# Turning q and k with SBUF-to-SBUF transfer transposes instead of on TensorE, with their casts one period earlier

## The chip, the cores and the metric

One core of one Trainium2 chip. The metric is the device time of one execution in microseconds (us). Before the change it was 352.41 us, the median of three runs (351.92 to 353.83). Runs over 1.5% above the fastest of the same kernel count as slow and are kept out of the ratios.

## The reference, cut to what matters

Attention of 8 heads over 8 batches of 576 tokens, with a window of 32 tokens to each side plus 8 global tokens, then a token-mixing and a channel-mixing MLP:

```python
scores = scale * np.matmul(q, k.transpose(0, 1, 3, 2))        # q, k, v: (8, 8, 576, 64) f32
mask = (np.abs(pos[:, None] - pos[None, :]) <= 32) | is_global[:, None] | is_global[None, :]
attn = softmax(np.where(mask, scores, -1e9));  x = attn @ v    # heads joined: (8, 576, 512)
h  = np.maximum(xt @ w_tok1, 0.0) @ w_tok2;    u = x + h.transpose(0, 2, 1)
h2 = np.maximum(u @ w_ch1, 0.0) @ w_ch2;       return u + h2   # w_ch1: 512 x 1536
```

## The kernel before

The work is cut into periods. In the period of batch b TensorE runs the channel MLP of b (the fixed work, `M4` and `M5`). Between its pieces it ends the attention of b+1 (`PV`, `M1`, `M2`, `M3`), and turns and scores q and k of b+2.

A score needs q and k with the head dimension on the partitions, while the load puts tokens there. So each pair of heads is loaded in f32, cast to f16 on ScalarE, turned on TensorE into PSUM (`T`), and copied by VectorE into token order (`TE`):

```python
def T(b, p):
    pT = (psm if b in (0, 2) else pss)([P, 2, 512], F16, name=f"pT_{b}_{p}")
    for ti, n in enumerate((qn, kn)):
        for i in range(4):
            nc.tensor.transpose(out=pT[:, ti, P*i : P*i+P], in_=n[b % 2][:, i, 2*p : 2*p+2, :], identity=ident)
    st[b]["pT", p] = pT
```

The load buffers `lq` and `lk` are single, the casts' outputs `qn` and `kn` double. The MLP's PSUM pool `psm` has two buffers, and ScalarE empties each with a Relu:

```python
def M4(b, j):                       # 12 groups of four matmuls per period
    ps = psm([P, 512], name=f"b1p_{b}_{j}")
    ... four matmuls ...
    nc.scalar.activation(out=s["b1"][:, j, :], in_=ps, func=AF.Relu)
```

And one queue, SyncE's, carries the q and k loads, the transposes of the MLP's input (`M3`) and the outputs:

```python
# first_half(b): n = b + 1, m = b + 2;  D is one piece of the fixed MLP work
u = [D, D, pv(0), D, pv(1), *c(0), D, pv(2), *c(1), D, pv(3), ..., *c(2), D]      # c(k): two casts of batch m
u += [pv(4), TR(m), *tt(0), *c(3), D, M1(n, 3), D, M1(n, 4), *c(4)]               # tt(p): T and TE of batch m
u += [load_v16(m), v_odd(m), globals_(m)]
u += [load_rest(m + 1), load_qk(m + 1)]                                           # used a period later
u += [*tt(1), D, D, M2(n, 0), M3(n, 0), D, M2(n, 1), M3(n, 1), *tt(2), D, M2(n, 2), ..., D]
```

The softmax here doesn't subtract the row's maximum and nothing guards it: scores larger than these inputs give would overflow.

## Time and profile before

| | before |
|---|---|
| time of the profiled run, span | 352.01 us, 350.2 us |
| mean granted TensorE clock (share of full speed that the chip allowed) | 0.984 |
| periods of batches 2, 3, 4, 5 | 38.0, 40.7, 35.6, 40.7 us |

A period is counted from the first MLP matmul (`b1p`) of a batch to that of the next. These two groups of the page are the ones to hold beside the changed kernel's (after the bar: busy us and mean ns of one, then the idle time ahead of the group and what ended it):

```profile
L739 PE MATMUL b1p<-uT,wc 128*128 128x512 f16 x384 | 95.6, 382 | 0.5 <-ACT b L742 0.5
...
L405 DVE COPY qT<-pT 128x512 f16<-128x512 f16 x30 | 20.6, 687 | 15.6 <-PE pT L399 15.4
```

Over the whole run TensorE waits 0.5 us for the Relu to empty a PSUM buffer. The Relu keeps up.

### The profile page before, as it was taken

Reading aid. Unit: us, or ns where it says so; the run is one execution under the profiler, and the core shown is the slowest. Engines: PE = TensorE matmul, PEld = TensorE weight load, DVE = VectorE, ACT = ScalarE, POOL = GpSimd, SP = SyncE. Lnnn points to the kernel's source line nnn. Section 1 sums busy time; section 2 is a strip of 40 time slices with the busy share of each in tenths; the row PEclk is TensorE's granted clock in tenths of the full one; section 3 lists DMA queues with packets and bytes.
Section 4 is the critical chain, followed back from the end, with each engine's and each line's share of the span. In section 5 each row is a group of like instructions: output and inputs, shape, how many; then the busy total and the mean of one; then the engine's idle time right before and its main releaser. Section 6 shows DMA issues by size and latency. Waiting matters only on the chain.

```text
span 350.2 us, 8086 instructions
## 1 busy us (share of the span) xinstructions
PE 319.4 (91%) x3431; PEld 174.0 (50%) x3431; DVE 190.4 (54%) x395; ACT 153.4 (44%) x275; POOL 86.8 (25%) x111
## 2 busy tenths in 40 slices
PE   4699998985899999799998999899989999999993
PEld 4357754443456544444454644444545645444641
DVE  7476576846742866456647475565656464241021
ACT  2460466025758044553475452554456433413600
POOL 5788686422126000520044001530000000000000
PEclk9999999997899999989999999999999999999999
DMA  6999999299857962929293922959100221042012
GB/s 199 216 155 263 249 128 70 92 226 204 255 60 70 256 139 65 93 60 287 92 89 56 257 92 66 96 162 214 62 2 19 73 72 52 0 105 92 0 68 86
DMA packets 82023, 42.38 MB, mean 121 GB/s; under 512 B 56578, under 2 KB 76674, under 8 KB 81986
## 3 DMA queue, kind: packets, MB, share of 16 engines
q1 hardware_dynamic: 44080, 31.34, 33.7%
q0 software_dynamic: 37904, 10.52, 28.1%
q8 instruction: 27, 0.44, 0.5%
q14 instruction: 10, 0.08, 0.1%
q10 hardware_dynamic: 2, 0.00, 0.0%
HBM read 36.11 MB, written 9.44 MB: 130 GB/s over the span
## 4 chain that ended last, share of the span: by engine, by line
PE 79%; DVE 8%; issue 5%; DMA 3%; ACT 2%; POOL 1%; SPq 1%; ACTq 0%
PE op L765 25%; PE b1p L739 23%; PE a1p L691 4%; PE pT L399 4%; PE hp L711 4%; PE s L457 4%; DMA lk<-in_k_dram 3%; PE b1lp L752 3%; PE pv L655 3%; PE pv L664 2%; DVE x L678 1%; PE a1p L612 1%; ACT e_all L469 1%; PE pv L586 1%; PE og L538 1%
## 5 line engine op out<-in xcount | busy, mean ns | idle before, releaser
L739 PE MATMUL b1p<-uT,wc 128*128 128x512 f16 x384 | 95.6, 382 | 0.5 <-ACT b L742 0.5
L742 ACT ACTIVATE b<-b1p 128x512 f16<-128x512 f32 x96 | 56.9, 598 | 88.1 <-PE b1p L739 87.9
L765 PE MATMUL op<-wc,b 128*128 128x512 f16 x384 | 89.3, 380 | 0.0
L469 ACT ACTIVATE e_all<-s 128x544 f16<-128x544 f32 (+1 forms) x64 | 41.0, 686 | 40.9 <-issue 30.5
L360 POOL DMA_DIRECT2D vsh<-in_v_dram x35 | 29.5, 853 | 118.2 <-PE pv L664 101.2
L765 PEld LDWEIGHTS <-b 128*128 128x128 f16 x384 | 35.3, 98 | 39.4
L739 PEld LDWEIGHTS <-wc 128*128 128x128 f16 x384 | 34.6, 98 | 37.4 <-issue 2.2
L769 DVE TENSOR_TENSOR osb<-u,op 128x512 f32<-128x512 f16 x32 | 22.0, 687 | 54.5 <-PE op L765 52.2
L405 DVE COPY qT<-pT 128x512 f16<-128x512 f16 x30 | 20.6, 687 | 15.6 <-PE pT L399 15.4
L716 DVE TENSOR_TENSOR u<-x,hp 128x1024 f16<-128x1024 f16 x14 | 17.0, 1220 | 21.3 <-PE hp L711 21.3
L677 DVE RECIPROCAL rr<-pv 128x8 f32<-128x8 f32 (+1 forms) x35 | 7.2, 206 | 33.3 <-PE pv L664 33.3
L480 DVE TENSOR_TENSOR e_all<-e_all,bandm 128x616 f16<-128x616 f16 x56 | 24.3, 475 | 1.0
L678 DVE TENSOR_TENSOR x<-pv,rr 128x512 f16<-128x512 f32 (+1 forms) x35 | 24.2, 691 | 1.2
L457 PE MATMUL s<-qT,kT 64*64 64x136 f16 (+2 forms) x704 | 19.4, 231 | 4.8 <-ACT kT L411 2.2
L457 PEld LDWEIGHTS <-kT 64*64 64x64 f16 x704 | 12.4, 114 | 19.2 <-issue 13.9
L411 DVE COPY kT<-pT 128x512 f16<-128x512 f16 x30 | 20.4, 680 | 1.5 <-PE pT L399 0.8
L711 PE MATMUL hp<-a,w 128*128 128x512 f16 x72 | 19.3, 386 | 1.5 <-ACT a L695 1.5
L399 PE MATMUL pT<-ident,qn 128*128 128x128 f16 x128 | 14.2, 241 | 6.9 <-DVE kT L437 6.3
L655 PE MATMUL pv<-rf,lf 128*64 128x264 f16 x126 | 18.9, 287 | 0.9 <-DVE kgz L354 0.7
L399 PE MATMUL pT<-ident,kn 128*128 128x128 f16 x128 | 14.5, 245 | 4.5 <-ACT kn L385 4.0
L664 PE MATMUL pv<-vsh,e_all 128*64 128x66 f16 x280 | 18.5, 194 | 0.0
L664 PEld LDWEIGHTS <-e_all 128*64 128x64 f16 x504 | 18.4, 111 | 0.0
(171 smaller groups left out, 383.8 us busy)
## 6 DMA issues: line engine op xcount, KB each, us to landing
out_dram<-osb SPq DMA_DIRECT2D x32, 256.0 KB
lq<-in_q_dram SPq DMA_DIRECT2D x6, 1024.0 KB
lk<-in_k_dram SPq DMA_DIRECT2D x6, 1024.0 KB
wc<-in_moe_w_ch_dram POOLq DMA_DIRECT2D x6, 512.0 KB, 7.7
vsh<-in_v_dram POOLq DMA_DIRECT2D x21, 128.0 KB, 5.0
vsh<-in_v_dram POOLq DMA_DIRECT2D x14, 96.0 KB, 3.0
lq<-in_q_dram SPq DMA_DIRECT2D x4, 256.0 KB
lk<-in_k_dram SPq DMA_DIRECT2D x4, 256.0 KB
```

What stands on the lines that cost most here:

```text
L360: nc.gpsimd.dma_start(out=vsh[b % 2][r0:r1, c, :, 0:D], in_=v[b, :, j0 : j0 + (r1 - r0), :].rearrange("h p d -> p h d"),)
L399: nc.tensor.transpose(out=pT[:, ti, P * i : P * i + P], in_=n[b % 2][:, i, 2 * p : 2 * p + 2, :], identity=ident)
L457: nc.tensor.matmul(ps[o, par, i0 - a : i1 - a], lhsT=kT[r, HQ * j : HQ * j + HQ], rhs=qf[r, i0:i1], start=b > 0, stop=b > 0 or j in js[-2:],)
L469: nc.scalar.activation(out=e2[:, :, a:z], in_=ps[:, :, 0 : z - a], func=AF.Exp, scale=scale)
L480: nc.vector.tensor_mul(out=e2[:, par], in0=e2[:, par], in1=bm)
L655: nc.tensor.matmul(ps[r0 : r0 + 64, hf, 0 : NP * VW], lhsT=s["lf"][:, HQ * t : HQ * t + HQ], rhs=s["rf"][:, 2 * hf : 2 * hf + 2], start=Tr ...
L664: nc.tensor.matmul(ps[r0 : r0 + 64, hf, VW * hh : VW * hh + VW], lhsT=e_all[:, h, lo : lo + HQ], rhs=(vod if t % 2 else vsh)[b % 2][:, tau ...
L678: nc.vector.tensor_tensor(out=x16s[b % 2][r, tau, :].rearrange("p (f h x) -> p f h x", f=2, h=NP), in0=pq[r, :, :, 0:D], in1=rr[r].unsquee ...
L711: nc.tensor.matmul(ps[:, i, :], lhsT=w2[:, ch, P * tau - sh : P * tau - sh + P], rhs=s["a1"][:, ch, :], start=(ch == 0), stop=(ch == 1),)
L739: nc.tensor.matmul(ps, lhsT=wc1[:, cc, P * j : P * j + P], rhs=s["uT"][:, cc, :], start=(cc == 0), stop=(cc == 3))
L742: nc.scalar.activation(out=s["b1"][:, j, :], in_=ps, func=AF.Relu)
L765: nc.tensor.matmul(ps, lhsT=w, rhs=wc2[:, j, :], start=(j == 0), stop=(j == NJ - 1))
```

## The change

For batches 4 to 7 the eight 128x128 transposes of a pair of heads leave TensorE. Eight DMA transposes per batch (`QT`) go from SBUF to SBUF instead, and VectorE puts the result in token order (`TS`). A transfer takes time to land, so the casts move from the period of the scores into the period ahead of it. The load behind them moves too, from the first half to the end of the second.

```diff
+    def QT(b, ti, i):
+        nc.sync.dma_start_transpose(
+            out=(qraw, kraw)[ti][:, :, i, :], in_=(qn, kn)[ti][b % 2][:, i].rearrange("p h d -> p (h d)"))
+    def TS(b, p):
+        nc.vector.tensor_copy(out=qTs[b % 2][:, p, 0:4, NG:QS]..., in_=qraw[:, p]...)
+        nc.vector.tensor_copy(out=kTs[b % 2][:, p, WIN : WIN + 512]..., in_=kraw[:, p]...)
 ... end of the stage before (sparse2) ...
+        u += [(0.0, c) for c in casts(n + 1)]
+        u += [(0.0, lambda ti=ti, i=i: QT(n + 1, ti, i)) for i in range(4) for ti in range(2)]
+        u += [(0.0, lambda: (load_rest(n + 2), load_qk(n + 2, slice(0, H))))]
 ... first_half(b) ...
-        cs = casts(m) if m < B else []
+        cs = casts(c_) if c_ < B else []          # c_ = b + 3
-            return [lambda: t(m, p)] if m < B else []
+            return [lambda: TS(m, p)] if m < B else []
-        if m + 1 < B:
-            u += [lambda: (load_rest(m + 1), load_qk(m + 1, slice(0, H)))]
 ... second_half(b) ...
-        return [D, s2(m, 0), D, lambda: t(m, 3), lambda: SM(m, 0), D, s2(m, 1), D, lambda: SM(m, 1), D, s2(m, 2), D, ...
+        return [D, *x(0), s2(m, 0), D, *x(1), lambda: SM(m, 0), D, s2(m, 1), *x(2), D, lambda: SM(m, 1), *x(3), D, s2(m, 2),
+                ld, D, ...                        # x(k): two QT of batch c_;  ld: the load of batch c_ + 1
```

More of the change, by code (lines that the diff above doesn't have):

```diff
@@ L418, in TE @@
         TEk(b, p)
+    qraw, kraw = [const.tile([P, NP, 4, P], F16, name=f"{n}raw") for n in "qk"]
+    def QT(b, ti, i):
+        nc.sync.dma_start_transpose(
+            out=(qraw, kraw)[ti][:, :, i, :], in_=(qn, kn)[ti][b % 2][:, i].rearrange("p h d -> p (h d)")
+        )
+    def TS(b, p):
+        nc.vector.tensor_copy(
+            out=qTs[b % 2][:, p, 0:4, NG:QS].rearrange("p t (x i) -> p t x i", i=4),
+            in_=qraw[:, p].rearrange("p i (t x) -> p t x i", t=4),
+        )
+        nc.vector.tensor_copy(
+            out=kTs[b % 2][:, p, WIN : WIN + 512].rearrange("p (x i) -> p x i", i=4),
+            in_=kraw[:, p].rearrange("p i x -> p x i"),
+        )
     def TR(b):
@@ L838, in first_half @@
     def first_half(b):
-        n, m = b + 1, b + 2
+        n, m, c_ = b + 1, b + 2, b + 3
         D = None
-        cs = casts(m) if m < B else []
+        cs = casts(c_) if c_ < B else []
         def c(k):
@@ L859, in first_half @@
             u += [lambda: (load_v16(m), v_odd(m)), lambda: globals_(m)]
-        if m + 1 < B:
-            u += [lambda: (load_rest(m + 1), load_qk(m + 1, slice(0, H)))]
         u += [*tt(1), D, D, lambda: (M2(n, 0), M3(n, 0)), D, lambda: (M2(n, 1), M3(n, 1)), *tt(2), D]
-        u += [lambda: (M2(n, 2), M3(n, 2) if n % 2 else None), D]
+        u += [lambda: (M2(n, 2), M3(n, 2) if n % 2 else None), D, *tt(3)]
         return u
     def second_half(b):
-        m = b + 2
+        m, c_ = b + 2, b + 3
         D = None
@@ L870, in second_half, with x, ld @@
             return []
-        return [D, s2(m, 0), D, lambda: t(m, 3), lambda: SM(m, 0), D, s2(m, 1), D, lambda: SM(m, 1), D, s2(m, 2), D,
-                lambda: SM(m, 2), lambda: GK(m), s2(m, 3), D, lambda: SM(m, 3), D, lambda: OG(m)]
+        def x(k):
+            return [lambda ti=ti: QT(c_, ti, k) for ti in range(2)] if c_ < B else []
+        def ld():
+            if c_ + 1 < B:
+                load_rest(c_ + 1)
+                load_qk(c_ + 1, slice(0, H))
+        return [D, *x(0), s2(m, 0), D, *x(1), lambda: SM(m, 0), D, s2(m, 1), *x(2), D, lambda: SM(m, 1), *x(3), D, s2(m, 2),
+                ld, D, lambda: SM(m, 2), lambda: GK(m), s2(m, 3), D, lambda: SM(m, 3), D, lambda: OG(m)]
     def dense(b):
```

## The prediction

> **What bounds the kernel now.** I read the page first, then the busy table by stage, the order of work on TensorE in one stage, and last ScalarE and the DMA queue of SyncE around the place where the change adds work.
>
> ```profile
> PE 319.4 (91%) x3431; PEld 174.0 (50%) x3431; DVE 190.4 (54%) x395; ACT 153.4 (44%) x275; POOL 86.8 (25%) x111
> PE 79%; DVE 8%; issue 5%; DMA 3%; ACT 2%; POOL 1%; SPq 1%; ACTq 0%
> ...
> 135.10:173.10 38.00, 35.66 (x378) 18.17 (x378) 23.13 (x49) 18.16 (x33) 8.07 (x7) 0.96 0.63 124
> 173.10:213.90 40.80, 39.29 (x439) 21.18 (x436) 23.49 (x44) 19.94 (x36) 8.08 (x7) 1.00 0.61 119
> 213.90:249.45 35.55, 33.89 (x376) 17.22 (x374) 21.54 (x42) 18.15 (x33) 8.07 (x7) 1.00 0.72 132
> 249.45:290.20 40.75, 39.24 (x435) 21.16 (x436) 21.92 (x44) 19.94 (x36) 0.00 (x0) 1.00 0.16 47
> ```
>
> TensorE holds the chain of waits (79%). The last four rows (length, busy of PE, PEld, DVE, ACT, POOL, clock, DMA share, GB/s) are the periods of batches 2 to 5, the ones that today turn q and k of batches 4 to 7. PE is idle in them for only 2.34, 1.51, 1.66 and 1.51 us. So only work or waits taken off TensorE can pay. Most of that idle time is one wait:
>
> ```profile
> 184.90 0.38 PE L399 MATMUL pT<-ident,qn 128*128 128x128 f16 x4 [1.51 <-DVE kT L437]
> 185.12 0.39 PE L399 MATMUL pT<-ident,kn 128*128 128x128 f16 x4
> 185.34 1.03 PE L739 MATMUL b1p<-uT,wc 128*128 128x512 f16 x4
> ```
>
> The first transposes of a batch wait for VectorE to empty the PSUM buffer of the rest rows, then four q and four k transposes hold PE from 184.90 to 185.34, 0.44 us.
>
> What the new order leans on, in the same trace:
>
> ```profile
> 132.67 1.27 ACT L469 ACTIVATE e_all<-s 128x544 f16<-128x544 f32 x2
> 136.21 0.60 ACT L742 ACTIVATE b<-b1p 128x512 f16<-128x512 f32 x1 [2.27 <-PE b1p L739]
> ...
> 139.07 0.40 ACT L382 CAST qr<-lqr 128x256 f16<-128x256 f32 x1
> 139.37 0.41 ACT L382 CAST kr<-lkr 128x256 f16<-128x256 f32 x1
> 140.15 0.60 ACT L742 ACTIVATE b<-b1p 128x512 f16<-128x512 f32 x1 [0.38 <-PE b1p L739]
> 140.64 0.61 ACT L385 CAST qn<-lq 128x512 f16<-128x512 f32 x1
> ```
>
> ```profile
> 139.49 0.70 SPq L120 DMA_DIRECT2D lqr<-in_q_dram  x1
> 140.29 0.65 SPq L120 DMA_DIRECT2D lkr<-in_k_dram  x1
> 154.34 0.41 SPq L116 DMA_DIRECT2D lq<-in_q_dram  x1
> 154.85 0.52 SPq L116 DMA_DIRECT2D lk<-in_k_dram  x1
> 157.01 6.02 SPq L728 DMA_TRANSPOSE uT<-u  x4
> ```
>
> ```profile
> 156.00:158.00 2.00, 1.00 0.97 284
> 158.00:160.00 2.00, 1.00 1.04 361
> 160.00:162.00 2.00, 1.00 1.10 349
> ```
>
> Casts and the Relu evictions of the MLP alternate on one in-order engine, so a cast that waits for its load holds up the evictions behind it. Today the load of 154.3 is used a period later (178.6), so it has 24 us. The last fence is that load on the wire (stretch, length, clock, DMA share, GB/s): some 350 GB/s until about 162. A DMA transpose takes 1.2 to 1.5 us of the SyncE queue.
>
> **What the Trainium skill says.**
> - "TensorE: Matmul & The Clock Gate", Part 4: PE-mode transpose, gives about 275 ns for a 128x128 transpose in a kernel. The rows here average 241 to 245 ns, but they are pipelined: 0.44 us for eight, 55 ns each. The 55 ns is what I remove.
> - "DMA: Bandwidth & Descriptors", Latency and other measured facts, has 261 GB/s and more for DMA transposes. This trace does not reach it: from 308 to 310, with transposes alone, it moves 130 GB/s, a 128 KB transpose per us or so. Issue sets the pace.
> - "VectorE: DVE Perf Modes", What auto-detection actually checks: a one-source copy with both sides in SBUF and even outer dimensions can take a two-port mode even with a step that is not 1. The f32 casts of that kind on VectorE (128x512) took 411 to 444 ns uncontended, against 680 to 687 for today's copies from PSUM. So I expect the new copies at 0.35 to 0.45 us.
> - "TensorE: Matmul & The Clock Gate", Why this matters for your kernels, warns of PE gaps over about 3 us. Here even the 1.66 us gap before 147.92 is followed by a granted clock of 0.50 for some 3.4 us (147.9 to 151.3), a loss of 1.7 us.
>
> **The change part by part.**
>
> Removed: 4 batches x 4 pairs x 8 transposes = 128 on TensorE. 16 groups x 0.44 us = 7.0 us of PE time, all in stages where PE sets the end. With them goes the wait of 1.5 us per period (1.51 in the row above; the next user of that PSUM buffer comes several us later): 4 x 1.5 = 6.0 us. Gross gain 3.3 us per period, 13 us in all.
>
> VectorE: 32 copies of 0.68 us from PSUM become 32 of about 0.4 us. VectorE is busy 23 of 38 us in these stages; worth nothing directly. Some will wait behind GpSimd's copies, as the copy of the global columns does now (1.73 us at 186.75 against 0.19 at 117.81); there are over 2 us of room before the next addition.
>
> ScalarE: the same casts, one period earlier. SyncE: 8 transposes more per period, 8 x 1.3 = 10.4 us of queue; the data, 1 MB at 130 GB/s, fits beside the rest.
>
> Moved, and this is the cost: loads. The load for a batch now stands on the SyncE queue behind the eight transposes of the batch before, while its casts are due early in the next period.
>
> At the end of the second stage: the last exponentials end at 133.94. The ten casts of batch 4 follow (2 x 0.3 + 8 x 0.51, start to start) to 138.7. Already the Relu of 136.21 slips to 138.8, so PE loses about 2 us, not yet counted since a longer stall follows. The transposes issue from 138.3 (all q casts done): 8 x 1.35 = 10.8, to 149.1. Then the two rest loads (0.75 + 0.65) and q and k (0.5 + 0.5): k issued by about 151.5. The load issued at 154.34 to 154.85 moved its 2.1 MB between 155 and about 162.3, so k landed some 7.2 us after the end of its issue; here that is 158.7. On ScalarE the cast of k of the first pair ends at 159.3, the Relu behind it at 159.9. TensorE has two PSUM buffers for the MLP: it fills them, then stands until about 153 (rest rows landed) and again until 159.9. The seventh MLP group (the one behind the second pair of casts) started at 148.93 before, in the chain of waits; it starts at 159.9, 11.0 later. Two long gaps cost another half-clock stretch of 1.7, as before the change; the later three transpose groups of this stage save 1.3. Period of batch 2: **+10.5**.
>
> Period of batch 3: its load leaves SyncE after eight transposes of the second half that themselves start after the five MLP transposes, some 4.3 us into that half. 4.3 + 8 x 1.3 + 2 outputs x 0.4 + loads 2.4 = 17.9 us in, where the half is about 13.3 long: 4.6 after the period's end. k lands at +11.8, its Relu is done at +13.0. The seventh MLP group stood at +12.25 (185.34): +0.75, less 1.3 of transposes, plus about 0.8 (half a chance of the 1.7 us clock loss): **+0.2**.
>
> Period of batch 4: no fifth MLP transpose, and the half is 3 us longer; the load leaves 1.3 before the end, k lands at about +6, when its cast is due. No stall: **-3.3**. Period of batch 5 has neither casts nor loads: **-3.3**.
>
> Sum: 10.5 + 0.2 - 3.3 - 3.3 = +4.1, so 352.4 becomes 356.5. I say 357, since every slip of the queue adds to it and none of the slack is counted twice.
>
> **The rivals.**
> 1. The loads come in time and the gross gain stays: 352.4 - 13.1 = 339. For it: DMA engines are idle half the time. Against it: the SyncE order itself, since the transposes need casts that cannot start before 133.9. I give it little.
> 2. The late load repeats in three periods rather than one and a bit, because transposes issue at 1.5 to 2.1 us (the four from 114.76 in the queue's order of time took 8.45): 8 x 0.5 = 4 us later each time, 361 to 364.
> 3. VectorE becomes the bound: strided copies slow, or stuck behind a transpose that has not landed. The transposes land some 5 us before their copies are due, and VectorE has 15 us idle per period. It would cost 1 to 3 us at most.
> 4. The first stall is shorter, transposes at 1.2 us and a load at 6.5: 2.5 less, 354, and with no stall for batch 3 about 352.
>
> **Range and chances.** The sum has one large positive term (8 to 14 us) and a sure negative one (6 to 8). That gives 351 to 363. Slower by over 2% needs over 359.5: the large term at its upper end, or rival 2; 0.28. Faster by over 2% needs rival 1: 0.05. Within: 0.67.
>
> **What would show it.** Right: PE waits in the early period of batch 2 released by the Relu on ScalarE, which idles for some 8 to 18 us on the loads of q and k; the stage from 135 about 10 us longer; the stages of batches 4 and 5 about 3.3 us shorter, with no wait on the rest rows' copy; copies at 0.35 to 0.45 us; transposes of q and k at 1.2 to 1.5 us of queue. Wrong: no ScalarE wait on a load in those stages (then near 339), or stalls of over 5 us in the periods of batches 3 and 4 too (then over 362).

## The result, and the profile after

The changed kernel took **369.67 us** (median of 4 runs, 366.47 to 371.78) against 353.12 us (4 runs, 351.92 to 354.13): ratio 1.0462, 95% interval 1.0359 to 1.0566, slower. A ratio here is the mean time of one kernel's fast runs over that of the other's of the same rounds, so it is not quite the ratio of the medians quoted. The prediction was 357, with 351 to 363 as its range: too low, and the result lies outside the range.

From the changed kernel's page, its busy line, its chain of waits by engine, and the MLP group:

```profile
PE 313.3 (85%) x3303; PEld 165.0 (45%) x3303; DVE 186.9 (51%) x395; ACT 153.8 (42%) x275; POOL 86.5 (23%) x111
...
PE 49%; DMA 19%; SPq 10%; DVE 8%; ACT 5%; issue 5%; POOL 1%; POOLq 0%; ACTq 0%; DVEq 0%
...
L756 PE MATMUL b1p<-uT,wc 128*128 128x512 f16 x384 | 101.0, 399 | 25.9 <-ACT b L759 25.8
```

There are 128 matmul records fewer, so TensorE has less work (313.3 us against 319.4). But its wait for the Relu went from 0.5 to 25.9 us, and the chain now runs 29% through transfers and SyncE's queue. The mean MLP matmul also rose, from 382 to 399 ns. The busy table by period of the changed kernel (batches 2 to 5; columns as in the prediction):

```profile
135.40:186.60 51.20, 36.76 (x350) 17.30 (x346) 24.37 (x49) 21.79 (x40) 8.15 (x7) 0.83 0.70 113
186.60:235.60 49.00, 40.62 (x402) 20.50 (x403) 21.02 (x44) 20.13 (x36) 8.08 (x7) 0.86 0.69 130
235.60:273.30 37.70, 34.00 (x344) 16.10 (x343) 20.27 (x42) 18.17 (x33) 8.08 (x7) 0.95 0.74 140
273.30:310.40 37.10, 37.10 (x403) 19.30 (x404) 21.05 (x44) 15.40 (x26) 0.00 (x0) 1.00 0.28 78
```

| period of batch | before | after | difference | predicted |
|---|---|---|---|---|
| 2 | 38.0 | 51.1 | +13.1 | +10.5 |
| 3 | 40.7 | 49.1 | +8.4 | +0.2 |
| 4 | 35.6 | 37.6 | +2.0 | -3.3 |
| 5 | 40.7 | 37.0 | -3.7 | -3.3 |
| sum | | | +19.8 | +4.1 |

The spans differ by 19.8 us (370.0 against 350.2), so these four periods hold all of it. The table also shows the only undisturbed one. In the last row TensorE is busy 37.10 of 37.10 us at clock 1.00: neither casts nor loads are left in that period, and the gain is there.

ScalarE in order of time shows the wait. The bracket is the idle time before the instruction and what ended it:

```profile
140.62 0.60 ACT L759 ACTIVATE b<-b1p 128x512 f16<-128x512 f32 x1 [0.62 <-PE b1p L756]
153.04 0.40 ACT L382 CAST qr<-lqr 128x256 f16<-128x256 f32 x1 [11.82 <-DMA lqr<-in_q_dram]
...
157.93 0.62 ACT L385 CAST qn<-lq 128x512 f16<-128x512 f32 x1 [2.96 <-DMA lq<-in_q_dram]
160.72 0.62 ACT L385 CAST kn<-lk 128x512 f16<-128x512 f32 x1 [2.17 <-DMA lk<-in_k_dram]
161.25 0.59 ACT L759 ACTIVATE b<-b1p 128x512 f16<-128x512 f32 x1
...
204.83 0.62 ACT L385 CAST kn<-lk 128x512 f16<-128x512 f32 x1 [3.84 <-DMA lk<-in_k_dram]
```

The Relu of 161.25 has long had its input. It stands behind casts that wait for a load. Until it is done the MLP's two PSUM buffers stay full, and TensorE stands (2.59 us before its group of 161.89). The last line is the same thing a period later. Why the loads are late is on SyncE's queue (start, duration of the issue):

```profile
138.52 1.21 SPq L423 DMA_TRANSPOSE qraw<-qn  x1
...
148.54 1.26 SPq L423 DMA_TRANSPOSE kraw<-kn  x1
...
151.79 0.57 SPq L116 DMA_DIRECT2D lk<-in_k_dram  x1
...
192.73 1.77 SPq L116 DMA_DIRECT2D lk<-in_k_dram  x1
...
236.46 0.57 SPq L116 DMA_DIRECT2D lk<-in_k_dram  x1
```

Eight transposes hold the queue from 138.52 to 149.80, and only then the loads go. From the end of k's issue to the start of its first cast it takes 8.4 us (152.36 to 160.72), then 10.3 (194.50 to 204.83), then 11.2 (237.03 to 248.25).

A third cost follows each stall. One MLP group of TensorE after the second stall, then the busy table of the stretch it starts:

```profile
206.00 1.87 PE L756 MATMUL b1p<-uT,wc 128*128 128x512 f16 x4 [6.20 <-ACT b L759]
```

```profile
206.00:211.90 5.90, 5.90 (x14) 2.08 (x14) 0.00 (x0) 4.17 (x8) 3.89 (x2) 0.50 0.06 4
```

Four matmuls take 1.87 us instead of some 1.03, and TensorE is busy all of 5.90 us at a granted clock of 0.50: about 3 us lost. The stretch after the first stall (161.9 to 167.6) loses another 2.9 in the same way. The clock had fallen before these stretches: to 0.50 at about 150.5, in the first long wait, and at about 198.3, after a wait of 2.18 us and before the second long one.

### The profile page after: what moved, and what is told of

It reads as the page before. It is cut to its first block, busy times and chain, and to the rows that moved or that the text cites.

```text
span 370.0 us, 7857 instructions
## 1 busy us (share of the span) xinstructions
PE 313.3 (85%) x3303; PEld 165.0 (45%) x3303; DVE 186.9 (51%) x395; ACT 153.8 (42%) x275; POOL 86.5 (23%) x111
## 4 chain that ended last, share of the span: by engine, by line
PE 49%; DMA 19%; SPq 10%; DVE 8%; ACT 5%; issue 5%; POOL 1%; POOLq 0%; ACTq 0%; DVEq 0%
PE op L782 18%; DMA lk<-in_k_dram 18%; PE b1p L756 16%; SPq L423 6%; PE a1p L708 3%; PE hp L728 3%; PE b1lp L769 3%; PE s L474 3%; DMA lv<-in_v_dram 2%; SPq L120 2%; PE pv L672 1%; ACT kn L385 1%; ACT e_all L486 1%; SPq L116 1%; PE pv L681 1%
## 5 line engine op out<-in xcount | busy, mean ns | idle before, releaser
L756 PE MATMUL b1p<-uT,wc 128*128 128x512 f16 x384 | 101.0, 399 | 25.9 <-ACT b L759 25.8
L756 PEld LDWEIGHTS <-wc 128*128 128x128 f16 x384 | 36.2, 101 | 69.0 <-issue 34.9
L782 PEld LDWEIGHTS <-b 128*128 128x128 f16 x384 | 35.5, 98 | 40.3
L474 PE MATMUL s<-qT,kT 64*64 64x136 f16 (+2 forms) x704 | 18.3, 224 | 7.8 <-DVE kT L411 3.0
L385 ACT CAST kn<-lk 128x512 f16<-128x512 f32 x25 | 15.6, 623 | 14.6 <-DMA lk<-in_k_dram 14.6
L474 PEld LDWEIGHTS <-kT 64*64 64x64 f16 x704 | 12.0, 111 | 21.1 <-issue 13.3
L385 ACT CAST qn<-lq 128x512 f16<-128x512 f32 x25 | 15.5, 619 | 13.6 <-DMA lq<-in_q_dram 13.6
L372 POOL COPY vod<-vsh 64x2112 f16<-64x2112 f16 x6 | 11.7, 1945 | 27.2 <-DMA vsh<-in_v_dram 27.2
L708 PE MATMUL a1p<-x,w 128*128 128x512 f16 x56 | 15.7, 408 | 0.0
## 6 DMA issues: line engine op xcount, KB each, us to landing
wc<-in_moe_w_ch_dram POOLq DMA_DIRECT2D x6, 512.0 KB, 11.1
```

What stands on the lines that cost most here:

```text
L385: eng(out=(qn, kn)[ti][b % 2][:, :, hs].rearrange("p i h d -> p h i d"), in_=(lq, lk)[ti][:, hs])
L474: nc.tensor.matmul(ps[o, par, i0 - a : i1 - a], lhsT=kT[r, HQ * j : HQ * j + HQ], rhs=qf[r, i0:i1], start=b > 0, stop=b > 0 or j in js[-2:],)
L708: nc.tensor.matmul(ps[tt], lhsT=w, rhs=x16s[b % 2][:, ch, :], start=(ch == 0), stop=(ch == NT - 1))
L756: nc.tensor.matmul(ps, lhsT=wc1[:, cc, P * j : P * j + P], rhs=s["uT"][:, cc, :], start=(cc == 0), stop=(cc == 3))
L782: nc.tensor.matmul(ps, lhsT=w, rhs=wc2[:, j, :], start=(j == 0), stop=(j == NJ - 1))
```

## The experiments

All twelve kernels computed the right result except one. Its output is wrong, which doesn't matter for the time. The profiled runs of the first, the fourth and the sixth (`e1`, `e4`, `e6`) fell in the slow state, so of `e1` and `e4` only the kind of wait is read, not the last microsecond. "Median" is of all runs, slow ones too; the ratios use fast runs alone, so compare by them. Periods are those of batches 2 to 5, from the profiled run.

| run | median (n) | before | ratio, 95% | periods 2 to 5 |
|---|---|---|---|---|
| e1_load_first | 362.93 (4) | 352.28 | 1.0169, 1.0016 to 1.0323 | 44.6 44.4 36.8 37.0 |
| e2_pe_turn_same_order | 360.06 (5) | 352.28 | 1.0196, 1.0073 to 1.0319 | 39.2 45.2 35.6 40.6 |
| e3_v_later | 371.27 (4) | 352.28 | 1.0464, 1.0305 to 1.0624 | 52.5 47.1 36.1 37.0 |
| e4_casts_late | 371.89 (4) | 352.28 | 1.0508, 1.0407 to 1.0610 | 44.3 50.2 42.1 37.0 |
| e5_turn_ahead_of_loads | 342.80 (6) | 351.26 | 0.9766, 0.9730 to 0.9801 | 34.5 38.5 34.6 37.0 |
| e6_pe_turn_casts_late | 351.58 (12) | 351.26 | 1.0004, 0.9970 to 1.0038 | 36.4 40.6 35.5 40.6 |
| e7_no_v (wrong result) | 365.70 (4) | 351.26 | 1.0384, 1.0315 to 1.0453 | 52.1 46.7 34.8 37.0 |
| e8_loads_on_act | 348.61 (17) | 351.26 | 0.9907, 0.9879 to 0.9935 | 44.1 37.9 33.1 37.0 |
| e9_keep_clock | 370.47 (4) | 351.26 | 1.0554, 1.0501 to 1.0608 | 51.8 48.2 36.7 37.0 |
| e10_copies_later | 339.83 (6) | 351.26 | 0.9688, 0.9648 to 0.9727 | 33.4 37.0 34.0 37.2 |
| e11_keep_clock_shorter | 367.13 (6) | 351.25 | 1.0438, 1.0381 to 1.0495 | 49.2 47.3 35.3 37.0 |
| e12_changed_again | 372.06 (6) | 352.40 | 1.0544, 1.0472 to 1.0615 | 52.3 49.8 36.4 37.0 |

My theory on reading the result: the loads are late because they stand on SyncE behind the transposes, and ScalarE's in-order casts carry that delay to TensorE. The rivals: the casts at their new place are dear by themselves, the v loads make the q and k loads slow to land, or most of the loss is TensorE's clock.

### e1: the loads ahead of the transposes

```diff
-        u += [QT(n + 1, ti, i) ...];  u += [load of n + 2]
+        u += [load of n + 2];  u += [QT(n + 1, ti, i) ...]
-        return [D, *x(0), s2(m, 0), ..., s2(m, 2), ld, D, ...
+        return [D, ld, *x(0), s2(m, 0), ..., s2(m, 2), D, ...
```

> The changed kernel with one edit: the loads of q and k for the batch after next are issued ahead of the eight transposes instead of behind them (end of the second stage, and start of each second half). My theory: the loss is the in-order wait of ScalarE's casts for loads that leave SyncE 10 us too late. Then the stalls of the periods of batches 3 and 4 vanish (they become some 37.5 and 32.2 us long), that of batch 2 shrinks by 8 to 10 us, and the time is 342 to 347 us. Rival A, the transposes themselves load the DMA engines and delay every load whatever the order: over 358. Rival B, the strided copies on VectorE hold the scores: no change, about 369.

It took 362.93 us (ratio 1.0169). The loss fell, but nowhere near what was expected. Among the waits from 180 to 232 (engine, tile and line, what it waited for: us in total, times, longest) are new ones:

```profile
DVE osb L786 <- DMA out_dram<-osb: 8.0, 2, 6.0
...
PE b1p L756 <- DVE osb L786: 5.4, 1, 5.4
```

Outputs share the queue, so with a big load ahead of them they leave late. Their three buffers then stay taken, VectorE waits for one, and TensorE waits for VectorE. The first transpose behind the load took 4.97 us to issue instead of 1.2. This is in keeping with the Trainium skill, "DMA: Bandwidth & Descriptors", Queues, rings and completion order: SyncE's issues share one row of rings, each consumed in order. So the loads' place matters, and moving them forward moves part of the wait. The expectation missed this.

### e2: the same order, TensorE turning

```diff
-            return [lambda: TS(m, p)] ...    and all QT
+            return [lambda: t(m, p)] ...     # T and TE on TensorE and VectorE, as before the change
```

> As the run above (loads first, casts one period ahead), but q and k of batches 4 to 7 are turned on TensorE with the copies from PSUM as in the kernel before; no SBUF transfer transposes of q and k. It measures what moving the transposes is worth by itself. My theory: 13 us slower than the run above (3.3 us per period of PE work and the wait on the rest rows' copy), so 355 to 360. Rival A, transfer transposes cost as much as they save: the same as the run above within 2 us.

360.06 us, not slower than e1 beyond the noise (1.0196 against 1.0169), where 13 us were expected. The period of batch 3 took 45.2 us without one q or k transfer transpose on the queue; there too VectorE waited for outputs to leave (3.6 us, and TensorE behind it 2.9). So the early load at that place is harmful by itself, whoever turns q and k, and the pair cannot measure what the transposes' move is worth; e5 and e6 do.

### e3: the v loads later

```diff
-            u += [lambda: (load_v16(m), v_odd(m)), lambda: globals_(m)]
+            u += [lambda: globals_(m)]                         # v moved to the start of second_half(b)
```

> The changed kernel with only the loads of v and their shifted copies moved from the first half to the start of the second half, away from the late loads of q and k. In the changed kernel k landed 8.9, 12.1 and 11.8 us after its issue instead of the 7.2 I reckoned with. If the v loads (small packets on the other queue) are what slowed it, k lands some 7.5 to 8.5 us after issue and the time falls by 5 to 10 us to 360 to 365. If the transposes ahead of it in the same queue slowed it, landing stays near 12 and the time within 2 us of 369.

371.27 us, no change. It tested nothing: the v loads are issued by GpSimd when their buffer comes free, and they went at about the same time (191.61 to 199.67, against 189.62 to 199.67 in the changed kernel). e7 is its replacement.

### e4: the casts late, the load and then the transposes at the end of the period

```diff
-        u = [..., *c(0), ..., *c(1), ...]                     # no casts in the first half
+        return [D, s2(m, 0), *cs(0), D, ..., *cs(4), D, ..., OG(m), ld, *x()]   # casts, load, eight QT
```

> The transfer transposes kept, but the casts of the next batch moved from the first half into the second half, loads next and transposes last, so that each load has a whole half period before its casts. My theory: no ScalarE wait on a load is left in the stages from batch 2 on, the gross gain of 13 us shows, less 1 to 3 us for the casts of batch 4 at the seam: 339 to 344. Rival A or B: at or over 352.

371.89 us. ScalarE no longer waits for q and k, yet nothing was won. Of the waits from 132 to 300:

```profile
DVE qT L428 <- DMA qraw<-qn: 33.0, 4, 12.5
...
PE hp L728 <- DVE u L733: 26.7, 3, 11.2
```

The wait went to the other end of the same queue. The transposes stand behind a load (the first took 4.84 us to issue), VectorE's copies wait for them, and the additions behind those copies hold up TensorE. Whichever of the two comes second on the queue is late for its in-order consumer.

### e5 and e6: transposes ahead of loads, and both with a period's time

Casts late as in e4, but the transposes go at the very start of the next period and the loads right behind them. So the load has until the second half before its casts are due. e6 is the control: the same order with TensorE turning.

```diff
+        def q8():
+            eight QT(m, ...)                    # e6: none
+            load_rest(c_); load_qk(c_)
-        u = [D, D, pv(0), D, pv(1), *c(0), ...
+        u = [q8, D, D, pv(0), D, pv(1), D, ...
+        u += [D, *tt(0), D, *tt(1), M2(n, 0), ...]     # tt: TS in e5, t in e6 (e6 keeps the old places)
```

> What the run with late casts showed: ScalarE no longer waited, but VectorE did, because the transposes stood behind 2 MB of loads in the same queue (single issues of 4.8 to 5.5 us). So here: casts of the next batch in the second half (those of batch 4 spread between the last scores of the second stage), the eight transposes at the start of the next period when no output transfer is due, and the loads behind them with some 10 us left before their casts. My theory now: any order in which neither ScalarE waits for a load, nor VectorE for a transpose or an output buffer, shows the whole gain: the periods of batches 2 to 5 are some 34.7, 37.4, 32.2 and 37.0 us against 38.0, 40.7, 35.6 and 40.7, and the time 338 to 343. Rival (transfer transposes cost somewhere else what they save): 350 or more.

> The same order of casts and loads as the run above, but q and k turned on TensorE with the copies from PSUM. If the gain of the run above comes from the transposes taken off TensorE, this one takes 350 to 354, with periods within 0.7 of those before the change. If it came from the new places of casts and loads, this one is as fast as the run above.

e5: 342.80 us. e6: 351.58, the same as before the change. So the new order alone is worth nothing (1.0004), the casts' place in the second half costs nothing, and the transposes' move is worth 8.8 us between these two. The time of e5 is at the upper end of what was expected: its periods of batches 3 and 4 took 38.5 and 34.6 us, not 37.4 and 32.2. e10 takes that up.

### e7: no v loads (wrong result)

```diff
-            u += [lambda: (load_v16(m), v_odd(m)), lambda: globals_(m)]
+            u += [lambda: v_odd(m), lambda: globals_(m)]
```

> The changed kernel with the loads of v left out from batch 4 on (wrong result on purpose: old rows of v are used). My run that moved them later in program order left them at the same times, so it did not test this. If the small packets of v slow the loads of q and k, k lands 7 to 8.5 us after the end of its issue in the periods of batches 3 and 4 (12.1 and 11.8 in the changed kernel), and the time falls to 358 to 364. If they do not, landing stays at 11 to 12 and the time at 367 to 371.

365.70 us, a relative error of 0.89, and between the two forecasts. (The 12.1 and 11.8 us of the expectation count from the start of k's issue, not from its end.) Counted so, k took 11.1 and 10.5 us to its cast in the periods of batches 3 and 4, about 1 us less than with the v loads. In that of batch 2 it took 10.5 against 8.9, so longer. That is no more than two profiles of one kernel differ. From the end of k's issue, e7 shows 9.9, 10.5 and 9.9 us, the changed kernel 8.4, 10.3 and 11.2, and the same kernel in e12 10.0, 13.0 and 10.6. The time's ratio, 1.0384, lies below the changed kernel's 1.0462 and 1.0544, but its interval (1.0315 to 1.0453) overlaps that of the first (from 1.0359). So the v loads may cost a little time, but that they slow k's landing is not shown, and what did is left open.

### e8: the changed kernel, its late loads on ScalarE's queue right behind the casts

```diff
-        ... s2(m, 2), ld, D, ...                                # second half, SyncE, behind eight QT
+        u += [lambda: (load_rest(c_ + 1, nc.scalar), load_qk(c_ + 1, slice(0, H), nc.scalar))]   # behind c(4)
```

> The changed kernel with the late loads issued from ScalarE's queue right behind the casts that free their buffer, so that they pass the SyncE queue with its eight transposes; everything else as changed. If SyncE's order is the cause, the stalls of batches 3 and 4 vanish and that of batch 2 shrinks by 8 us: 343 to 350. What may stay is the wait of output buffers behind the transposes (up to 2 us per period). If loads and transposes only share the wires, so that order does not matter: 360 or more.

348.61 us. Casts, transposes and copies are those of the changed kernel; only where the loads stand differs, on the other queue and so much earlier. k's issues for the periods of batches 3 and 4 ended at 158.60 and 194.05, not at 194.50 and 237.03. These periods fell from 49.1 and 37.6 us to 37.9 and 33.1. One wait for a load is left, at the first one, which has no period to land in (that wait, then an early issue):

```profile
150.35 0.62 ACT L385 CAST kn<-lk 128x512 f16<-128x512 f32 x1 [5.06 <-DMA lk<-in_k_dram]
...
158.12 0.48 ACTq L116 DMA_DIRECT2D lk<-in_k_dram  x1
```

This is the plainest test: loads that do not stand behind the transposes leave early, and the stalls of batches 3 and 4 are gone. In these periods it also clears the casts' place in the change, which e8 keeps. In that of batch 2 (44.1 us against 38.0 before) the early casts still cost, since they come before any load could land.

### e9, e11 and e12: the clock

Matmuls that nobody reads keep TensorE busy in the gaps of the changed kernel, so that the clock stays up. e12 is the changed kernel once more, to see how far a second measurement differs.

```diff
+    def fill(b, k):
+        ps = psv([P, P], name=f"fill_{b}_{k}")
+        for _ in range({(2, 0): 150, (2, 1): 25, (3, 1): 55, (4, 1): 25}.get((b, k), 0)):   # e9: 130, 90, 100, 60
+            nc.tensor.matmul(ps, lhsT=ident, rhs=ident, start=True, stop=True)
```

> The changed kernel with dummy matmuls (128x128, result unread) put where TensorE stands in the periods of batches 2 to 4: 130 and 90, 100, and 60 of them, to fill most of each gap and keep the granted clock. The changed kernel ran 17.1, 13.7 and 3.4 us at half clock there, by my reckoning with a loss of some 2.9 + 3.0 + 1.7 us of busy time after the gaps. If that is right the time falls by 5 to 8 us to 362 to 365. If the half clock costs nothing because TensorE waits anyway: within 1.5 us of 369.7. If the fill overshoots the gaps, the time rises.

> The filled run again with fewer dummy matmuls behind the second wait (25, 55 and 25; 150 behind the first), since there they ended 3.4 and 2.3 us after the Relu that TensorE was waiting for. The half clock was gone in that run (3.4 + 3.4 us instead of 34), but what it gave was eaten by the overshoot. If the half clock costs the changed kernel what I reckon (2.9 us in the period of batch 2, 3.0 in that of batch 3, 1.7 in that of batch 4), this run takes 362 to 366. If the clock is worth nothing: 369 to 371.

> The changed kernel as it is, once more in five rounds, to have its level and its periods a second time beside those of the edited ones: ratio to the kernel before 1.045 to 1.050 (the first measurement gave 1.0462 with a wide interval), periods of batches 2 to 5 within 2 us of 51.1, 49.1, 37.6 and 37.0. If its periods come out 2 us shorter each in this profile, what the filled run gained on the half clock was only the spread of the profiles.

e9 brought the stretches at half clock from 34.2 us down to 6.8 in the periods of batches 2 to 4. But its fills ran 3.4, 1.7 and 3.4 us past the end of the Relu that was awaited (the expectation of e11 names two of these, 3.4 and 2.3), and it took 370.47 us. e11's shorter fills took 367.13 us, just over the 362 to 366 expected, against 372.06 for e12. e12's ratio, 1.0544, is above its expected 1.045 to 1.050. The ratios of e11 and e12, 1.0438 and 1.0544, have intervals that overlap (up to 1.0495, from 1.0472), and that of the changed kernel's first measurement, 1.0462, lies between. By period e11 is 3.1, 2.5 and 1.1 us shorter than e12. But counted from the period's start, k's cast came 1.1 us later in e12 in the period of batch 2 and 1.9 us later in that of batch 3, which leaves about 3.7 us for the clock. Against the first profile of the changed kernel the same count gives about 4.1. So the half clock is worth some 4 us by these profiles: a part of the loss, not most of it, and not shown beyond the noise of the times.

### e10: e5 with the copies behind the additions

```diff
-        u += [D, *tt(0), D, *tt(1), M2(n, 0), D, M2(n, 1), *tt(2), D, ...]
+        u += [D, D, M2(n, 0), *tt(0), D, M2(n, 1), *tt(1), D, M2(n, 2), *tt(2), D]     # TS(m, 3) in the second half
```

> The fast version (transposes at the period's start, loads behind them, late casts) with VectorE's copies from the raw tiles moved behind the additions that TensorE waits for: pair 0 and 1 after the first and second addition, pair 2 after the third, pair 3 after the first output. In the fast version the copies waited up to 3.0 us for a transpose or for GpSimd's lock and pushed back the additions (TensorE waited 3.8 us in all on them). Expected: periods of batches 3 and 4 near 37.4 and 32.3 (38.5 and 34.6 there), time 338.5 to 341. If those waits were not on the path: the same 342.8 within 1.

339.83 us, the best, faster than both kernels (0.9688). Its groups by line (`--lines`) have the copies, and its busy table the periods of batches 2 and 3:

```profile
L428 DVE COPY qT<-qraw 128x512 f16<-128x512 f16 x16 | 9.6, 599 | 0.1
```

```profile
136.96:170.37 33.41, 32.09 (x350) 15.72 (x345) 20.98 (x49) 18.58 (x34) 8.07 (x7) 1.00 0.95 172
170.37:207.35 36.98, 36.98 (x409) 19.27 (x403) 21.24 (x45) 19.92 (x36) 8.08 (x7) 1.00 0.98 159
```

TensorE is idle for 1.32 and 0.00 us, at full clock. The four periods are 4.6, 3.7, 1.6 and 3.5 us shorter than before the change, 13.4 in all. (That of batch 4 took 34.0 us where 32.3 was expected.) Part of this only moved: the casts of batch 4 now stand in the stage ahead, which ends 1.9 us later (136.96 against 135.07). The whole span is 11.9 us shorter (338.3 against 350.2). e5's copies had stood ahead of an addition that TensorE waits for, on an in-order VectorE, and some had waited for their transposes; behind it they have time.

## Why the prediction was wrong

**What held.** The mechanism was the predicted one: ScalarE's casts wait for loads that stand behind the transposes, the Relu behind them holds TensorE, and half clock follows. Seven of each eight transposes took 1.20 to 1.34 us of the queue, as said. The gross gain of 13 us is nearly real too: 13.4 in the four periods of e10, 11.9 over its span. Rival 1 (339) describes e10's time, but it needed another order. The last period gained 3.7 us where 3.3 was said. Of its own signs of being wrong, "stalls of over 5 us in the periods of batches 3 and 4 too", the first came true (6.20 us at 206.00), the second in a smaller size (3.38 at 249.41).

**What failed** is the sum's positive side: how late the loads land. Three terms were too small.

1. *"k landed some 7.2 us after the end of its issue".* It was taken from a load that had the wire nearly to itself. (By the lines shown, 162.3 less the end of k's issue at 155.37, it was in fact 6.9.) Here it was 8.4, 10.3 and 11.2 us to the cast that waits. What makes the difference was not separated (rest rows, v loads, outputs, transposes still on the wire).
2. *The queue's slip.* "8 x 1.3 + 2 outputs x 0.4 + loads 2.4" was 13.6 us and took 16.6 for batch 3 (177.87 to 194.50), with one transpose of 2.70 us and k's issue of 1.77. For batch 4, "the load leaves 1.3 before the end ... No stall" was the plain failure: k's issue ended 1.4 us after the period's start. So a stall stood there as well. Part of this was arithmetic: 17.9 less one transpose of 1.3, in a half of 13.3 + 3, puts the load 0.3 us behind the end, not 1.3 ahead of it. I counted lone issues back to back; rival 2, which had the stall repeat in three periods through slow transposes, came nearest. But only one transpose of each eight was slow (2.1 to 2.7 us), and its 361 to 364 was still too low.
3. *The clock.* 1.7, 0.8 and 0 us were entered; the stretches show about 2.9, 3.0 and, behind a stall of 3.38 us at 249.41, 1.7.

The terms given for batch 2 don't make its +10.5 as they stand: 11.0 less 1.3 is 9.7, and with the 1.7 of clock 11.4. And 8 to 14 less 6 to 8, on 352.4, spans 352 to 360, so the range of 351 to 363 had a margin in it. From the parts, as an estimate: period 2 has k's cast 1.7 us later than predicted (counted from the period's start) and 1.2 us more of clock, 2.9 where 2.6 is missing. Period 3 has 3.4 us of later issue, 3.1 of landing and 2.2 of clock, 8.7 where 8.2 is missing. Period 4 has the 3.38 us stall and 1.7 of clock, 5.1 where 5.3 is missing. So some 11.6 us of the missing 15.7 is the loads and 5.1 the clock, with an overlap of about a microsecond. e8 shows the loads' part on the chip; e11 is in keeping with the clock's part, but not clear of the noise.

**The copies** were expected at 0.35 to 0.45 us and took 599 ns (q) and 596 ns (k) on the average in e10, about 0.5 us start to start. Some were held far longer. In the changed kernel, VectorE first, then GpSimd at the same time:

```profile
162.31 2.34 DVE L432 COPY kT<-kraw 128x512 f16<-128x512 f16 x1
```

```profile
162.18 2.03 POOL L373 COPY vod<-vsh 64x2112 f16<-64x2112 f16 x1 [0.24 <-DMA vsh<-in_v_dram]
```

The Trainium skill, "SBUF — State Buffer", Who interferes with whom, says that a VectorE copy in a two-port mode and GpSimd exclude each other for a whole instruction. The trace agrees: 2.34 us beside a GpSimd copy of 2.03, against 0.58 for the same copy at 165.20. It cost nothing: TensorE was then busy at half clock. Rival 3 (VectorE the bound) did not come about.

**What the prediction should have done**: ask, for every load that moves behind other work on a queue, how far its issue can slip before its consumer waits. The slack was put at 1.3 us in one period and was negative in another, and a slip of about 3 us on a shared queue left a stall in both.

## What to carry to other kernels

Taking work off the bounding engine paid here only once what replaces it no longer pushed a load past its due time on a shared queue. What worked: put the transposes ahead of the loads at the start of a period, and give the load the rest of the period before an in-order engine casts it. When a reordering only moves a wait from one engine to another (ScalarE in the change, VectorE in e1 and e4), look for the queue they have in common. Test the new order without the change (e6 against e5) to see what each is worth.

## What the Trainium skill lacked or had wrong

- "DMA: Bandwidth & Descriptors" gives a bandwidth for DMA transposes, but no time that one of a given size holds its queue on this chip (only sequencer cycles for "previous generations", in its part on trn3). Here a 128 KB transpose held SyncE's queue for 1.20 to 1.34 us, one of each eight for 2.1 to 2.7, and the first behind a q and k load for 3.2 to 5.5 us (e1 and e4, profiled in slow runs). That set the order of everything.
- The same page has no figure for a load's time from issue to landing with other transfers beside it: here 8.4 to 13.0 us from the end of k's issue to its cast (the changed kernel, profiled twice), against some 7 where little else ran. A rule for sharing one queue among loads, transposes and outputs would have helped: an output behind a load cost VectorE 6.0 us in one wait (e1, in a slow run).
- "VectorE: DVE Perf Modes" says when a copy can take a two-port mode, but has no figure for a 16-bit copy within SBUF that reorders its elements. My 0.35 to 0.45 us came from f32 casts; the runs show 599 ns on the average, 0.5 us start to start, and 2.34 us beside a copy of GpSimd.
- "TensorE: Matmul & The Clock Gate" warns of gaps over about 3 us. Before the change, a gap of 1.66 us (ended at 147.92) came with a stretch of 3.4 us at half clock, while an equal gap (ended at 225.81) came with none: the clock of that period is 1.00. So the length of one gap did not decide here. In the changed kernel the clock fell at about 198.3, after a gap of 2.18 us; a longer one of 6.20 us followed, and then 5.90 us of work at 0.50.
